# Full 128x128 matmuls for scores and AV of batches 1 to 3, with block-diagonal queries and zero-padded exponentials

## The chip, the cores and the metric

One core of a Trainium2 chip runs the whole program. The metric is the time of one execution on the device in microseconds (us). Its engines work side by side, each through its own instructions in program order, and wait for one another by semaphores: TensorE (PE, with its weight loads as PEld), VectorE (DVE), ScalarE (ACT), GpSimd (POOL) and SyncE (SP), which here only issues DMAs.

## The reference

Sparse attention over 4 batches of 8 heads, 768 positions of 64 elements, and then a feed-forward layer with a gated activation. Each query sees the keys closer than 16 positions, and one summary per block of 32 keys: the block's maximum as key and its mean as value.

```python
k_sum = k.reshape(B, H, nb, block, D).max(axis=3)      # block 32, nb 24
v_sum = v.reshape(B, H, nb, block, D).mean(axis=3)
scores_l = scale * q @ k.T                             # kept where |i - j| < 16
scores_s = scale * einsum('bhsd,bhnd->bhsn', q, k_sum) + log(block)
a = softmax(concatenate([scores_l, scores_s]))
x = (a @ concatenate([v, v_sum])).transpose(0, 2, 1, 3).reshape(B * S, H * D)
h = x @ w_in                                           # 512 -> 2048
out = (h * sigmoid(beta * h)) @ w_out                  # 2048 -> 512
```

q, k, v and the weights come as float32; the matmuls run in bfloat16.

## The kernel before

Two heads share the 128 partitions, 64 elements each, so the 8 heads are 4 pairs (`g`). Queries are cut into 12 tiles of 64 (`QT`), six in each half `u`. For a tile, the 96 keys of its window and the 24 summary keys make one set of 120 rows, held in `kw[g]` with 128 columns per tile. Scores stand transposed, keys on partitions: `s` in a PSUM bank, 128 x 768 for a pair and a half. ACT takes the exponential into `e` (`weigh`), DVE multiplies by the band mask (`mask_e`), and AV uses the tile of `e` as weights against the values `ve` (even tiles) and `vo` (odd tiles, the same values shifted by 64 rows), with a column of ones that gives the sum. `norm` divides on DVE (a reciprocal and a multiplication) into `xn`; `x_dma` transposes that by DMA, issued on ACT, into `xT`. `vm_all` computes the block means on PE, `spread` copies them on DVE into the lower rows of `ve` and `vo`.

The feed-forward layer takes most of PE. `h_tile` and its like multiply by `w_in` (L600), and the multiplication by `w_out` runs as seven products of half-size blocks (`product`, L664) whose operands are differences and sums formed on DVE: `t_sb` of the weights, `s_sb` of h (`h_sums`, `tt` at L645). `gather` adds the products up into `o_sb`, and SP stores it.

The order is written out. A list `main` holds the steps of the feed-forward layer: the h of batch 0 in two halves, its output, then for batches 1 to 3 the h (16 steps) and the products (21 steps). `run` walks it and puts in side steps, each at a position from the table `AT` (4.754 is behind step 4). The attention of batch b + 1 runs as side steps of the output of batch b. Batch 1 has its queries and keys turned on PE (`qt_pe`, copied out by L371 on DVE and L368 on ACT); in batches 2 and 3 loads, casts to bf16 on POOL (`kq_cast`, through the buffers `nat`) and transposing DMAs on SP (`kq_dma`) bring them into `qn[g]` and `kT[g]`.

PSUM is divided into two single banks `one`, three pairs of banks `big`, which while products run become two more accumulators (`acc`) and two of `big`. Scores of half 0 go into `big[2]`, of half 1 into `big[1]`; AV of pair g goes into `big[1 + g % 2]`. `e` has eight buffers.

In scores, each head is a matmul of its own with 64 partitions (L439, in batch 1; L436 in the other two), in AV each tile has weights of 128x64 and writes a half of the output's partitions (L511). Batch 0 has steps of its own (`HEAD`).

Of the kernel before, what the change touches and what calls it, by code (L numbers as in the profile page):

```python
# [17 lines left out]
    'clear': [6.428, 6.644],  # L18
# [3 lines left out]
    'late': [32.254],  # L22
# [5 lines left out]
    'sc1': [28.05, 28.06, 30.05, 30.06, 31.438, 31.448, 33.219, 33.904],  # L28
    'mk1': [28.082, 28.092, 30.899, 30.909, 32.558, 32.75, 33.826, 34.448],
    'silu1': [34.957],  # L30
    'vm1': [30.622],
    'sp1': [31.039, 33.384],
    'av1': [35.473, 35.88, 37.299, 37.483],
    'xd1': [36.323, 36.794, 40.874, 39.001],
# [14 lines left out]
    'sc2': [64.902, 64.912, 67.132, 67.349, 69.423, 69.507, 71.144, 71.507],  # L49
    'mk2': [64.907, 67.547, 69.019, 69.041, 70.656, 70.74, 74.611, 74.621],  # L50
    'silu2': [83.261],
    'vm2': [69.738],
    'sp2': [70.773, 71.834],
    'av2': [73.1, 73.251, 76.15, 76.759],
    'xd2': [73.535, 75.753, 77.844, 80.713],
# [14 lines left out]
    'sc3': [100.954, 100.964, 104.012, 104.199, 106.253, 106.263, 107.654, 107.71],  # L70
    'mk3': [101.397, 102.413, 107.921, 107.97, 106.952, 108.221, 108.907, 110.666],
    'silu3': [112.501],
    'vm3': [107.308],
    'sp3': [107.454, 109.743],
    'av3': [110.088, 110.664, 114.187, 114.973],
    'xd3': [111.756, 114.644, 117.265, 117.799],
# [4 lines left out]
    'mask2': [46.27],  # L81
# [21 lines left out]
def kernel(  # L103
# [10 lines left out]
    nc = tc.nc  # L114
    ctx.enter_context(tc.manual_schedule())
    P = 128
# [8 lines left out]
    W = 16  # L125
# [17 lines left out]
    NEG = -30000.0  # L143
    assert d_model == H * D and out.shape == (B * S, d_model) and NK + nb <= P
# [104 lines left out]
    mask = const.tile([P, NT, QT], bf16, name="mask")  # L249
# [600 lines left out]
    def av_two(g, u, ts):  # L850
        for i, t in enumerate(ts):
            av_mm(0, g + i, u, t[:, 0])
# [116 lines left out]
```

## Time and profile before

| | us |
|---|---|
| median of 3 runs (lowest, highest) | 216.38 (216.24, 218.27) |
| span of the profiled execution | 213.4 |
| PE busy in that span | 202.9 (95%) |
| weight loads busy | 140.1 (66%) |
| DVE busy | 139.5 (65%) |
| ACT busy | 119.0 (56%) |
| POOL busy | 62.0 (29%) |

The span goes from the first to the last instruction that the profiler saw; the run's time includes what lies around it, so the median of the runs is 3.0 us above the span. The profile gives no other time of its own for that execution. Batch 1's attention lies at about 55 to 75 us, batch 2's at 100 to 123, and batch 3's at 145 to 168.

In a row of the timeline stand start, time, engine, line, operation, written and read tile, shape, and the number of instructions that the row merges; in brackets how long the engine had been idle and what released it. Neighbouring matmuls overlap, so that the time of a row of eight is longer than the distance to the next row.

### The profile page before, as it was taken

The page shows a single profiled execution, that of the slowest core. Times are in us where ns is not written, and L with a number is a line of the kernel's source. Part 1 is how long each engine was busy: PE and PEld are TensorE (multiplying, and loading weights), DVE is VectorE, ACT ScalarE, POOL GpSimd, SP SyncE. Part 2 cuts the span into 40 slices and gives each one's busy share as a digit, 9 for nine tenths or more (in the row PEclk, how much of TensorE's full clock was granted, in tenths as well). Part 3 has the DMA queues.
Part 4 walks back from the last instruction along what each step waited for, and adds up shares of the span by engine and source line. Part 5 has one row for each costly group of instructions (what it writes and reads, how often), then busy time and mean ns, then how long its engine had stood idle before and what let it go on. Part 6 is the DMA issues. An engine that isn't in the chain of part 4 may idle for free.

```text
span 213.4 us, 5774 instructions
## 1 busy us (share of the span) xinstructions
PE 202.9 (95%) x2393; PEld 140.1 (66%) x2393; DVE 139.5 (65%) x323; ACT 119.0 (56%) x182; POOL 62.0 (29%) x94
## 2 busy tenths in 40 slices
PE   7778999999998999999999999999999999999993
PEld 2366856565554586556888875667788855668882
DVE  4297574799839992677889920999789704464232
ACT  2246986579489121966883137778772229772210
POOL 7609990002620009423520153461600100000111
PEclk9999999999999999999999999999999999999999
DMA  6998999999877995999979999999834820000242
GB/s 119 183 219 150 185 207 207 206 208 214 113 187 199 243 202 179 236 152 202 170 152 223 194 272 272 210 193 194 123 129 27 185 99 3 0 0 3 98 98 98
DMA packets 78393, 33.92 MB, mean 159 GB/s; under 512 B 60688, under 2 KB 75424, under 8 KB 78368
## 3 DMA queue, kind: packets, MB, share of 16 engines
q1 hardware_dynamic: 61968, 23.92, 55.2%
q0 software_dynamic: 7424, 7.34, 21.4%
q10 hardware_dynamic: 8976, 2.30, 7.3%
q8 instruction: 18, 0.29, 0.6%
q14 instruction: 7, 0.06, 0.1%
HBM read 27.37 MB, written 6.29 MB: 158 GB/s over the span
## 4 chain that ended last, share of the span: by engine, by line
PE 54%; DVE 14%; DMA 14%; SPq 5%; ACT 4%; issue 4%; POOL 3%; POOLq 0%; DVEq 0%
PE big L600 18%; PE one L664 11%; PE acc L664 8%; DMA vst<-in_v_dram 8%; PE big L578 4%; PE one L615 3%; DMA krow<-in_k_dram 3%; ACT e L447 3%; DVE kw L371 2%; DVE w_out_sb L337 2%; DMA qst<-in_q_dram 2%; DVE km L357 2%; DVE e L451 2%; POOL ve L456 1%; SPq L210 1%
## 5 line engine op out<-in xcount | busy, mean ns | idle before, releaser
L600 PE MATMUL big<-xT,w_in_sb 128*128 128x384 bf16 x360 | 60.5, 326 | 0.0
L600 PEld LDWEIGHTS <-w_in_sb 128*128 128x128 bf16 x384 | 37.5, 98 | 25.1 <-issue 0.7
L611 ACT ACTIVATE h_sb<-big,beta_sb 128x768 bf16<-128x768 f32 x45 | 39.6, 904 | 25.7 <-PE big L600 25.6
L664 PEld LDWEIGHTS <-h_sb 128*128 128x128 bf16 x320 | 30.6, 98 | 4.9 <-issue 0.5
L645 POOL TENSOR_TENSOR o_sb<-p,u 128x256 f32<-128x256 f32 x10 | 7.3, 727 | 88.9 <-DVE u L645 77.0
L447 ACT ACTIVATE e<-big,bias 128x768 bf16<-128x768 f32 x32 | 27.3, 900 | 6.2 <-PE big L426 4.3
L664 PE MATMUL one<-w_out_sb,h_sb 128*128 128x256 bf16 x240 | 30.4, 273 | 0.2 <-ACT p L368 0.2
L664 PEld LDWEIGHTS <-s_sb 128*128 128x128 bf16 x240 | 23.2, 98 | 2.8
L645 DVE TENSOR_TENSOR s_sb<-h_sb 128x768 bf16<-128x768 bf16 (+2 forms) x16 | 7.8, 487 | 23.5 <-ACT h_sb L611 23.5
L645 DVE TENSOR_TENSOR u<-one,p 128x256 f32<-128x256 f32 x20 | 8.4, 422 | 15.8 <-PE one L664 15.5
L456 POOL CAST ve<-vst 128x832 bf16<-128x832 f32 (+2 forms) x16 | 14.1, 901 | 14.9 <-DMA vst<-in_v_dram 12.5
L368 ACT COPY o_sb<-one 128x256 f32<-128x256 f32 (+1 forms) x14 | 6.1, 433 | 18.4 <-PE one L664 10.0
L451 DVE TENSOR_TENSOR e<-e,mask 128x768 bf16<-128x768 bf16 x24 | 13.7, 597 | 3.9 <-ACT e L447 3.6
L615 PE MATMUL one<-w_out_sb,h_sb 128*128 128x512 bf16 x64 | 15.2, 380 | 0.0
L365 POOL COPY kw<-km 128x288 bf16<-128x288 bf16 x12 | 7.5, 628 | 24.1 <-DVE km L357 14.4
L361 DVE TENSOR_REDUCE km<-kT 128x24 bf16<-128x768 bf16 x12 | 11.2, 944 | 1.8 <-ACT kT L368 1.8
L538 DVE TENSOR_TENSOR xn<-big,r 128x768 bf16<-128x768 f32 x12 | 11.5, 957 | 0.4
L578 PE MATMUL big<-xT,w_in_sb 128*128 128x384 bf16 x64 | 11.7, 327 | 0.0
L664 PE MATMUL acc<-t_sb,h_sb 128*128 128x256 bf16 x80 | 10.9, 273 | 0.0
L568 POOL CAST qn<-qst 128x768 bf16<-128x768 f32 x8 | 7.4, 938 | 10.2 <-DMA qst<-in_q_dram 6.9
L664 PE MATMUL one<-t_sb,s_sb 128*128 128x256 bf16 x80 | 10.4, 273 | 0.0
L664 PE MATMUL acc<-t_sb,s_sb 128*128 128x256 bf16 x80 | 10.4, 273 | 0.0
(145 smaller groups left out, 309.1 us busy)
## 6 DMA issues: line engine op xcount, KB each, us to landing
out_dram<-o_sb SPq DMA_DIRECT2D x19, 256.0 KB, 2.7
vst<-in_v_dram SPq DMA_DIRECT2D x13, 336.0 KB, 5.1
kst<-in_k_dram SPq DMA_DIRECT2D x8, 384.0 KB, 5.0
qst<-in_q_dram SPq DMA_DIRECT2D x8, 384.0 KB, 4.6
w_in_sb<-in_moe_w_in_dram POOLq DMA_DIRECT2D x4, 512.0 KB, 8.0
w_out_sb<-in_moe_w_out_dram POOLq DMA_DIRECT2D x4, 512.0 KB, 13.1
vo<-ve SPq DMA_DIRECT2D x12, 107.2 KB, 2.4
vst<-in_v_dram SPq DMA_DIRECT2D x3, 416.0 KB, 7.1
```

The source lines that it names most:

```text
L361: nc.vector.tensor_reduce(out=km[g][:, NK:NK + nb], in_=kT[g][:, W:W + S].rearrange("p (n f) -> p n f", f=block), op=ALU.max, axis=AX.X)
L365: eng.tensor_copy(out=kw[g][:, :, NK:NK + nb], in_=km[g][:, None, NK:NK + nb].to_broadcast([P, NT, nb]))
L447: nc.scalar.activation(out=e[:], in_=s[:, :, 0:HS], func=ACTF.Exp, bias=bias[:, 0:1], scale=scale)
L451: nc.vector.tensor_mul(out=e.rearrange("p h (m q) -> p h m q", q=QT), in0=e.rearrange("p h (m q) -> p h m q", q=QT), in1=(mask2 if b > 1 e ...
L456: eng.tensor_copy(out=ve[:, g, lo:hi, 0:D], in_=vst[g][:, lo:hi])
L538: nc.vector.tensor_mul(out=x[:, 3 * us[0]:3 * us[0] + 3 * n].rearrange("p (k j) h d -> p k (j h) d", k=n), in0=tv[:, :, :, 0:D], in1=r[:, ...
L578: nc.tensor.matmul(t[:, 0:HS], w_in_sb[:, ki, i * P:(i + 1) * P], xT[:, ki, 0:HS], start=(ki == 0), stop=(ki == k1 - 1))
L600: nc.tensor.matmul(o, w_in_sb[:, ki, i * P:(i + 1) * P], x, start=(ki == 0), stop=(ki == k1 - 1))
L611: nc.scalar.activation(out=o, in_=t, func=ACTF.Silu, scale=beta_sb[:, i:i + 1])
L615: nc.tensor.matmul(t[:, 0:hi - lo], h_sb[:, n, ms * P:(ms + 1) * P], w_out_sb[:, n, lo:hi], start=(n == 0), stop=(n == k2 - 1))
L645: eng.tensor_tensor(out=o, in0=a, in1=b, op=op)
L664: nc.tensor.matmul(SLOTS[n], a[:, j, t * P:(t + 1) * P], b[:, j], start=(j == 0 and n not in (2, 3, 7)), stop=(j == J2 - 1), skip_group_ch ...
```

## The change

Scores become one matmul for both heads. A tile `qz` of 128 x 2 x 4 x 768 holds the queries block-diagonally: copy 0 has the first head in partitions 0 to 63 and zeros below, copy 1 the second head in partitions 64 to 127 and zeros above. The weights are all 128 rows of `kw` for the tile, the 128 columns of the moving side are 64 queries of one head and 64 of the other. `qn[g]` is now a view of copy 0.

The exponentials live in five fixed tiles `epad` of 6 x 3 x 64: the middle block of each three is zero. AV takes as weights 128 columns that begin with the even tile and end in zeros, or begin with zeros and end with the odd tile, so that both add up in the same full output. The tiles are handed out from a list `free_e` and given back where AV has been issued.

So that `qz` is filled, `qt_pe` copies half a partition range at a time, alternately by DVE and ACT, and turns into `big[1]` and `big[0]`. In batches 2 and 3 the transposing DMA still writes both heads into copy 0; `q_fix` then moves the second head into copy 1 (DVE) and clears its place (POOL). Zeros are set by a memset at the start, by `clear_q` (two memsets of 64 x 1536) and by `clear_e`. The mask has 14 tiles instead of 12, ordered for the new layout, and its turned copy for batches 2 and 3 (`turn_mask`) is made ahead of batch 1 (position 6.9 instead of 46.27). The pools `nat` and `op` go from 5 to 4 and from 4 to 3 buffers, and the eight buffers of `e` go. Positions in `AT` of scores, masks, means, spreads, AV and `x_dma` change, mostly to earlier ones, and AV of one pair now stands among the scores of later pairs; `qf2` and `qf3` are new.

```diff
@@ AT (a few of its lines) @@
-    'clear': [6.428, 6.644],
+    'clear': [5.9, 6.644, 6.9, 6.1, 7.2, 7.3],
...
-    'sc2': [64.902, 64.912, 67.132, 67.349, 69.423, 69.507, 71.144, 71.507],
+    'sc2': [64.902, 64.912, 66.6, 66.61, 69.423, 70.5, 71.8, 72.6],
...
-    'av2': [73.1, 73.251, 76.15, 76.759],
+    'av2': [70.1, 71.6, 73.9, 75.8],
...
-    'mask2': [46.27],
+    'qf2': [58.2, 59.6, 60.6, 66.9],
+    'qf3': [94.5, 95.5, 95.9, 97.5],
@@ -141,14 +142,14 @@
     k2 = d_ff // P
     VW = D + 2
     NEG = -30000.0
+    NE = 5
     assert d_model == H * D and out.shape == (B * S, d_model) and NK + nb <= P
 
     const = ctx.enter_context(tc.tile_pool(name="consts", bufs=1))
     stage = ctx.enter_context(tc.tile_pool(name="stage", bufs=7))
-    natp = ctx.enter_context(tc.tile_pool(name="nat", bufs=5))
-    ep = ctx.enter_context(tc.tile_pool(name="ep", bufs=8))
+    natp = ctx.enter_context(tc.tile_pool(name="nat", bufs=4))
     xp = ctx.enter_context(tc.tile_pool(name="xp", bufs=4))
-    op = ctx.enter_context(tc.tile_pool(name="op", bufs=4))
+    op = ctx.enter_context(tc.tile_pool(name="op", bufs=3))
     ps = ctx.enter_context(tc.tile_pool(name="ps", bufs=1, space=bass.MemoryType.PSUM))
 
     one = [ps.tile([P, 1, 512], f32, name=f"one{i}") for i in range(2)]
...
-    mask = const.tile([P, NT, QT], bf16, name="mask")
+    mask = head.tile([P, NT + 2, QT], bf16, name="mask")
...
@@ -292,16 +293,23 @@
     select(band[:], 2 * W - 1, [[1, QT]], -1)
 
     def more_masks():
-        nc.vector.tensor_copy(out=mask[:], in_=band[:, None, :].to_broadcast([P, NT, QT]))
-        nc.vector.memset(mask[0:W, 0], 0.0)
-        nc.gpsimd.affine_select(out=mask[:, NT - 1], in_=mask[:, NT - 1], compare_op=ALU.is_ge, fill=0.0,
-                                base=QT + W - 1, pattern=[[0, QT]], channel_multiplier=-1)
+        nc.vector.tensor_copy(out=mask[:], in_=band[:, None, :].to_broadcast([P, NT + 2, QT]))
+        nc.vector.memset(mask[0:W, 0:2], 0.0)
+        nc.gpsimd.affine_select(out=mask[:, NT:], in_=mask[:, NT:], compare_op=ALU.is_ge, fill=0.0,
+                                base=QT + W - 1, pattern=[[0, 2], [0, QT]], channel_multiplier=-1)
         nc.vector.memset(mask[NK:NK + nb], 1.0)
 
-    mask2 = const.tile([P, NT, QT], bf16, name="mask2")
+    mask2 = const.tile([P, NT + 2, QT], bf16, name="mask2")
 
     def turn_mask():
         nc.vector.tensor_copy(out=mask2.rearrange("p m (c f) -> p m c f", c=2), in_=mask.rearrange("p m (f c) -> p m c f", c=2))
+
+    def clear_q(gs):
+        nc.vector.memset(qz[D:P, 0, gs], 0.0)
+
+    def clear_e():
+        for t in epad:
+            nc.vector.memset(t[:, :, 1], 0.0)
 
     def clear_kw():
         for g in range(G):
@@ -309,7 +317,10 @@
             nc.vector.memset(kw[g][:, NT - 1, QT + W:NK], 0.0)
             nc.vector.memset(kw[g][:, :, NK + nb:P], 0.0)
 
-    qn = [const.tile([P, S], bf16, name=f"qn{g}") for g in range(G)]
+    qz = const.tile([P, 2, G, S], bf16, name="qz")
+    qn = [qz[:, 0, g] for g in range(G)]
+    epad = [const.tile([P, 2 * 3, 3, QT], bf16, name=f"ep{i}") for i in range(NE)]
+    nc.vector.memset(qz[0:D, 1], 0.0)
...
-    def qt_pe(b, gs, bg, cps):
+    def qt_pe(b, gs, bg):
         ts = [turned(qrow, b, big[bg][:, i], g) for i, g in enumerate(gs)]
-        for g, t, cp in zip(gs, ts, cps):
-            cp(qn[g].rearrange("p (f c) -> p f c", c=CS[b]), t.rearrange("p c f -> p f c"))
+        for g, t in zip(gs, ts):
+            for h, cp in enumerate((dve_cp, act_cp)):
+                r = slice(h * D, (h + 1) * D)
+                cp(qz[r, h, g].rearrange("p (f c) -> p f c", c=CS[b]), t[r].rearrange("p c f -> p f c"))
+
+    def q_fix(g):
+        nc.vector.tensor_copy(out=qz[D:P, 1, g], in_=qz[D:P, 0, g])
+        nc.gpsimd.memset(qz[D:P, 0, g], 0.0)
 
 
     et, turns = {}, {}
 
     def q_tile(g, h, m):
         return qn[g][h * D:(h + 1) * D, m * QT:(m + 1) * QT]
-
...
@@ -430,26 +443,40 @@
         s = big[bg]
         for j in range(HT):
             m = u * HT + j
-            for h in range(2):
-                o = s[:, h, j * QT:(j + 1) * QT]
-                if b > 1:
-                    nc.tensor.matmul(o.rearrange("p (c f) -> p c f", c=2), kw[g][h * D:(h + 1) * D, m, :], q_tile2(g, h, m),
-                                     start=True, stop=True)
-                else:
-                    nc.tensor.matmul(o, kw[g][h * D:(h + 1) * D, m, :], q_tile(g, h, m), start=True, stop=True)
+            o, q = s[:, j % 2, j // 2 * P:(j // 2 + 1) * P], qz[:, :, g]
+            if b > 1:
+                o = o.rearrange("p (h c f) -> p h c f", h=2, c=2)
+                q = q.rearrange("p h (j c f) -> p h j c f", c=2, f=P)[:, :, m // 4, :, m % 4 * 32:m % 4 * 32 + 32]
+            else:
+                o = o.rearrange("p (h f) -> p h f", h=2)
+                q = q[:, :, m * QT:(m + 1) * QT]
+            nc.tensor.matmul(o, kw[g][:, m, :], q, start=True, stop=True)
         turns["s", g, u] = s
         weigh(b, g, u)
 
+    free_e = list(range(NE))
+
+    def release(b, g, u):
+        free_e.append(et.pop((b, g, u))[0])
+
     def weigh(b, g, u):
         s = turns.pop(("s", g, u))
-        e = ep.tile([P, 2, HS], bf16, name="e", tag="e")
-        et[(b, g, u)] = e
-        nc.scalar.activation(out=e[:], in_=s[:, :, 0:HS], func=ACTF.Exp, bias=bias[:, 0:1], scale=scale)
+        n = free_e.pop(0)
+        t = epad[n]
+        if b == 0:
+            e = t.rearrange("p a b q -> p (a b q)")[:, 0:2 * HS].rearrange("p (h s) -> p h s", h=2)
+            o, i = e, s[:, :, 0:HS]
+        else:
+            e, o, i = t, blocks(t), s[:, :, 0:HS].rearrange("p b (a q) -> p b a q", q=QT)
+        et[(b, g, u)] = n, e
+        nc.scalar.activation(out=o, in_=i, func=ACTF.Exp, bias=bias[:, 0:1], scale=scale)
+
+    def blocks(t):
+        return t[:, :, 0:3:2].rearrange("p a b q -> p b a q")
 
     def mask_e(b, g, u):
-        e = et[(b, g, u)]
-        nc.vector.tensor_mul(out=e.rearrange("p h (m q) -> p h m q", q=QT), in0=e.rearrange("p h (m q) -> p h m q", q=QT),
-                             in1=(mask2 if b > 1 else mask)[:, None, u * HT:(u + 1) * HT, :].to_broadcast([P, 2, HT, QT]))
+        e = blocks(et[(b, g, u)][1])
+        nc.vector.tensor_mul(out=e, in0=e, in1=(mask2 if b > 1 else mask)[:, 2 * u:2 * u + NT].rearrange("p (b a) q -> p b a q", b=2))
 
 
     def v_cast(eng, g, lo=0, hi=JV):
@@ -500,9 +527,9 @@
     xn = {}
     AVW = 3 * 2 * (D + 1)
 
-    def av_mm(b, g, u, t):
+    def av_mm0(g, u, t):
         tv = t[:, 0:AVW].rearrange("p (j h e) -> p j h e", j=3, h=2)
-        e = et[(b, g, u)]
+        e = et[(0, g, u)][1]
         for j in range(3):
             J = 3 * u + j
             for h in range(2):
@@ -510,10 +537,21 @@
                     lo = (2 * j + par) * QT
                     nc.tensor.matmul(tv[par * QT:(par + 1) * QT, j, h], e[:, h, lo:lo + QT],
                                      (vo if par else ve)[:, g, h * J6 + J, 0:D + 1], start=True, stop=True)
+        release(0, g, u)
+
+    def av_mm(b, g, u, t):
+        tv = t[:, 0:AVW].rearrange("p (j h e) -> p j h e", j=3, h=2)
+        e = et[(b, g, u)][1].rearrange("p a b q -> p a (b q)")
+        for j in range(3):
+            for h in range(2):
+                for par in range(2):
+                    nc.tensor.matmul(tv[:, j, h], e[:, 2 * j + h, par * QT:par * QT + P],
+                                     (vo if par else ve)[:, g, h * J6 + 3 * u + j, 0:D + 1], start=(par == 0), stop=(par == 1))
+        release(b, g, u)
 
...
...
@@ -902,12 +941,11 @@
     at("av0", [lambda: av_two(0, 1, one), lambda: av_two(2, 1, one[1:]), lambda: av_two(3, 1, one[:1])])
     at("x0", [lambda: x_two(0, 1, dve_cp, one[0]), lambda: x_two(2, 1, dve_cp, one[1])])
     at("scale", [lambda i=i: scale4(i) for i in range(4)])
-    at("clear", [clear_kw, more_masks])
+    at("clear", [clear_kw, more_masks, turn_mask, clear_e, lambda: clear_q(slice(0, 2)), lambda: clear_q(slice(2, 4))])
     at("kt", [lambda i=i: kt_pe(1, (2 * i, 2 * i + 1), 1 + i, dve_cp) for i in range(2)])
     at("km", [lambda g=g: km_pe(g, nc.gpsimd) for g in range(G)])
-    at("qt", [lambda i=i: qt_pe(1, (2 * i, 2 * i + 1), 1 + i, (dve_cp, act_cp)) for i in range(2)])
+    at("qt", [lambda i=i: qt_pe(1, (2 * i, 2 * i + 1), 1 - i) for i in range(2)])
     at("late", [late_tiles])
-    at("mask2", [turn_mask])
...
+            at("qf" + n, [lambda g=g: q_fix(g) for g in range(G)])
             at("win" + n, [lambda g=g: windows_nat(dve_cp, g) for g in range(G)])
             at("kx" + n, [lambda g=g: key_max_nat(g) for g in range(G)])
             at("ks" + n, [lambda g=g: key_sums(nc.gpsimd, g) for g in range(G)])
```

Three places show how instructions move. The first is DVE ahead of batch 1's first masks. Before (`big1` and `big2` hold turned queries, `e_1156` is the first tile of exponentials):

```order
L645 TENSOR_TENSOR t_sb_189<-w_out_sb_184 128x2048
L357 TENSOR_REDUCE km3_130<-kw3_119 128x24
L645 TENSOR_TENSOR t_sb_189<-w_out_sb_184,t_sb_189 128x2048
L371 COPY qn0_177<-big1_80 128x768
L371 COPY qn2_179<-big2_81 128x768
L451 TENSOR_TENSOR e_1156<-e_1156,mask_111 128x768
L451 TENSOR_TENSOR e_1170<-e_1170,mask_111 128x768
```

Now, with `ep4_179` as the first tile of exponentials:

```order
L684 TENSOR_TENSOR t_sb_189<-w_out_sb_184 128x2048
L368 TENSOR_REDUCE km3_127<-kw3_116 128x24
L684 TENSOR_TENSOR t_sb_189<-w_out_sb_184,t_sb_189 128x2048
L382 COPY qz_174<-big1_77 64x768 x2
L382 COPY qz_174<-big0_82 64x768 x2
L479 TENSOR_TENSOR ep4_179<-ep4_179,mask_108 128x2x6x64
```

Two copies of whole query pairs have become four of half the partitions, and ACT has the other four. Further up on DVE, between the masks and the scaling of `w_out`, stands the turned mask and the clearing of `qz`:

```order
L296 COPY mask_108<-band_107 128x896
L297 MEMSET mask_108 16x64
L300 MEMSET mask_108 24x896
L305 COPY mask2_173<-mask_108 128x896
L308 MEMSET qz_174 64x768 x2
L348 TENSOR_SCALAR w_out_sb_184<-w_out_sb_184,inv_beta_186 128x512 x4
```

Before, the rows L296 to L300 stood there as L295 to L299, with `w_out`'s scaling directly behind them.

The second place is PE in batch 1, where AV of a pair ends. Before, behind AV of pair 1 in `big2`:

```order
L511 MATMUL big2_81<-ve_120,e_1209 64x65
L511 LDWEIGHTS e_1209
L511 MATMUL big2_81<-vo_121,e_1209 64x65
L615 LDWEIGHTS h_sb_182
L615 MATMUL one1_79<-w_out_sb_184,h_sb_182 128x512
```

Now, behind AV of pair 0 in `big1`:

```order
L548 MATMUL big1_77<-ve_117,ep2_177 128x65
L548 LDWEIGHTS ep2_177
L548 MATMUL big1_77<-vo_118,ep2_177 128x65
L453 LDWEIGHTS kw2_115
L453 MATMUL big1_77<-qz_174,kw2_115 128x128
```

The products that stood behind AV stand later; the scores of pair 2 (`kw2`) follow, into the bank into which AV has just written.

The third place is DVE in batch 2, at the last sums of h that the products need. Before:

```order
L645 TENSOR_TENSOR s_sb_1302<-h_sb_182 128x768
L645 TENSOR_TENSOR s_sb_1302<-s_sb_1302,h_sb_182 128x768
L645 TENSOR_TENSOR s_sb_1302<-h_sb_182,s_sb_1302 128x768
L645 TENSOR_TENSOR h_sb_182<-h_sb_182 128x2x384
L371 COPY kw2_118<-kT2_125 128x12x96
L361 TENSOR_REDUCE km2_129<-kT2_125 128x24
```

Now:

```order
L382 COPY kw2_115<-kT2_122 128x12x96
L415 COPY qz_174<-qz_174 64x768 x2
L372 TENSOR_REDUCE km2_126<-kT2_122 128x24
L684 TENSOR_TENSOR s_sb_1388<-h_sb_182 128x384
L684 TENSOR_TENSOR s_sb_1388<-s_sb_1388,h_sb_182 128x384
L684 TENSOR_TENSOR s_sb_1388<-h_sb_182,s_sb_1388 128x384
```

The copies of L415 are `q_fix`; two of them stand between the keys' copy and their maximum, ahead of the last sums. The first of them stands ahead of the third group of sums.

More of the change, by code (lines that the diff above doesn't have):

```diff
@@ L21 @@
     'qt': [26.508, 26.967],
-    'late': [32.254],
+    'late': [35.9],
     'ws': [23.447, 26.164, 38.352, 39.431],
@@ L570, in kq_dma @@
     def kq_dma(nm, b, g):
-        t = kT[g][:, W:W + S] if nm == "k" else qn[g][:]
+        t = kT[g][:, W:W + S] if nm == "k" else qn[g]
         nc.sync.dma_start_transpose(out=t.rearrange("p (j t) -> p j t", j=J6),
```

38 lines of the change are left out of this document (18 added, 20 removed).

## The prediction

> **What bounds the kernel now.** I read the busy shares first, then the stretches around the edited work, then the waits of TensorE, then the timelines.
>
> ```profile
> span 213.4 us, 5774 instructions
> PE 202.9 (95%) x2393; PEld 140.1 (66%) x2393; DVE 139.5 (65%) x323; ACT 119.0 (56%) x182; POOL 62.0 (29%) x94
> 50.00:58.00 8.00, 7.98 (x98) 4.37 (x96) 8.00 (x14) 4.81 (x8) 3.68 (x5) 1.00 1.09 156
> 58.00:81.00 23.00, 21.75 (x326) 13.86 (x325) 17.95 (x38) 12.47 (x20) 2.58 (x5) 1.00 0.87 195
> 100.00:116.00 16.00, 16.00 (x282) 12.99 (x280) 14.57 (x34) 11.82 (x19) 5.08 (x6) 1.00 0.89 183
> 140.00:160.00 20.00, 19.83 (x301) 14.88 (x298) 16.98 (x37) 15.28 (x23) 6.79 (x9) 1.00 0.88 160
> PE big L439 <- ACT qn L368: 0.6, 1, 0.6
> PE big L439 <- ACT e L447: 0.4, 1, 0.4
> PE big L511 <- DVE e L451: 0.2, 1, 0.2
> ```
>
> The stretches list length, then busy time of PE, weight loads, DVE, ACT and POOL. TensorE bounds everything: it is 95% busy, and in the stretches that hold the scores and the AV of batches 2 and 3 it loses 0.0 of 16 and 0.2 of 20 us. Its waits at the edited instructions come to 1.2 us in all. So there is nearly nothing to win in waits, and whatever new wait TensorE gets is paid in full. DVE has no slack from 50 to 58 us, where batch 1 begins: it is busy 8.00 of 8.00.
>
> **Term 1: TensorE's own work.** Three rows of TensorE's timeline (start, time, instructions), then three pieces of the chain:
>
> ```profile
> 105.42 1.04 PE L664 MATMUL one<-w_out_sb,h_sb 128*128 128x256 bf16 x8
> 106.39 0.52 PE L436 MATMUL big<-qn,kw 64*128 64x64 bf16 x24
> 106.84 1.05 PE L664 MATMUL one<-w_out_sb,h_sb 128*128 128x256 bf16 x8
> 68.60 0.88 PE big L511 x48
> 167.67 0.33 PE big L560 x6
> 23.71 0.19 PE one L519 x6
> ```
>
> Eight products take 0.87 when others follow. From 105.42 to 106.84 are 1.42, so 24 small score matmuls, which serve two steps, cost 0.55, with about 0.10 of change-over in it. They become 12 with 128x128 weights and 128 columns; six such (L560) take 0.33, so 0.66: +0.11, twelve times, +1.3. AV: 48 small matmuls, two head pairs, take 0.88, so one pair 0.49 with its change-over; it becomes 24 with full weights and 65 columns, six of which (L519) take 0.19: 0.74. +0.25, twelve times, +3.0. Sum **+4.3**; ends 2 (no change-over saved, weight loads hidden better) and 5.
>
> **Term 2: the start of batch 1.** Before:
>
> ```profile
> 38.14 0.56 DVE L371 COPY xT<-one 128x768 bf16<-128x768 bf16 x1 [0.72 <-PE one L860]
> 56.20 1.81 DVE L371 COPY qn<-big 128x768 bf16<-128x768 bf16 x2
> 57.18 1.66 ACT L368 COPY qn<-big 128x768 bf16<-128x768 bf16 x2 [2.86 <-DVE qn L371]
> 58.73 0.59 ACT L368 COPY o_sb<-one 128x512 f32<-128x512 f32 x1
> 59.28 1.69 ACT L447 ACTIVATE e<-big,bias 128x768 bf16<-128x768 f32 x2
> 61.18 0.52 PE L439 MATMUL big<-qn,kw 64*128 64x64 bf16 x24
> L304 DVE COPY mask<-mask 128x768 bf16<-128x768 bf16 x1 | 0.6, 550 | 0.0
> L232 DVE MEMSET blank<- 128x256 uint32 x1 | 0.3, 272 | 0.9 <-PEq L953 0.9
> L261 DVE MEMSET edge<- 128x128 uint32 x1 | 0.2, 165 | 0.0
> ```
>
> DVE gets, ahead of the query copies: the mask turn 0.57 (it stood after batch 1, and is 896 wide now), two clears of qz of 768 words (0.272 and 0.165 at 256 and 128 words give 0.7 each, 1.35), and the widened mask 0.2. Five clears of e (192 words, 0.2 each) fall almost wholly into DVE's idle time ahead of the two xT copies (0.72 in this row); 0.2 is left of them and of hand-overs. Together +2.3, and no slack to take it. The copies then begin at 58.5. They become eight halves that differ in partitions, not in elements per lane, so each keeps its 0.95 (DVE) or 0.80 (ACT); each ACT half waits for DVE's, and DVE's second for ACT's first, as all write qz. Two such ladders end near 58.5 + 6.3 = 64.8. The o_sb copy follows on ACT, and the first exponentials run 65.3 to 67.1. Scores of pair 1, at 61.18 before, wait for each of the two banks in turn: 66.25 and 67.1 instead, with nothing else of TensorE between. **+6.0**. Ends: 3 (the additions alone, with a little handing over) and 7.
>
> **Term 3: scores behind the norm.** The diff's order puts scores of pair 2 directly behind AV of pair 0 in the same bank, and scores of pair 3 directly behind AV of pair 1. A bank must be normalised before it is overwritten:
>
> ```profile
> 115.32 0.23 DVE L537 RECIPROCAL r<-big 128x12 f32<-128x12 f32 x1
> 115.58 0.96 DVE L538 TENSOR_TENSOR xn<-big,r 128x768 bf16<-128x768 f32 x1
> 112.45 0.63 DVE L496 COPY vo<-vm_sb 32x768 bf16<-32x768 bf16 x2
> ```
>
> That is 1.2, with 0.25 of hand-overs 1.45, while TensorE has nothing it may run. A mask (0.6) or the two spreads (1.2) ahead on DVE make it 2.0 to 2.65. Walking DVE's new order: batch 1 1.45 and 2.4, batch 2 2.0 and 1.7, batch 3 2.65 (once; there AV follows the scores). **+10.2**; ends 6 and 12.
>
> **Term 4: AV behind the last exponentials.**
>
> ```profile
> 104.14 1.70 ACT L447 ACTIVATE e<-big,bias 128x768 bf16<-128x768 f32 x2
> L451 DVE TENSOR_TENSOR e<-e,mask 128x768 bf16<-128x768 bf16 x24 | 13.7, 597 | 3.9 <-ACT e L447 3.6
> 116.57 1.28 ACTq L553 DMA_TRANSPOSE xT<-xn  x1
> ```
>
> The exponential of the last step (0.85) and its mask (0.6) stand behind an issue of xT on ACT (1.28), which now lies between the exponentials of pair 3. AV of pair 2 comes after a few products, and waits 1.3, 1.6 and 1.0 in the three batches, **+3.9**; ends 1 and 5.
>
> **Term 5: means and spreads.**
>
> ```profile
> L645 DVE TENSOR_TENSOR u<-one,p 128x256 f32<-128x256 f32 x20 | 8.4, 422 | 15.8 <-PE one L664 15.5
> ```
>
> The value means follow product 7 directly, into the bank that the product's sum still fills, and wait for DVE's u and o_sb (0.42 each) and what is ahead: 2.15 and 1.95 in batches 2 and 3. The first AV waits for the spreads: 1.35, 0.3 and 1.05. **+6.8**; ends 3 and 8.
>
> **Term 6: q_fix ahead of the sums.**
>
> ```profile
> 100.33 2.76 SPq L572 DMA_TRANSPOSE qn<-qn  x2
> qn<-qn SPq DMA_TRANSPOSE x8, 3.5
> 103.28 0.36 DVE L645 TENSOR_TENSOR s_sb<-h_sb,s_sb 128x384 bf16<-128x384 bf16 x1
> 103.66 1.05 PE L664 MATMUL one<-t_sb,s_sb 128*128 128x256 bf16 x8
> 140.12 3.89 SPq L572 DMA_TRANSPOSE qn<-qn  x3
> L361 DVE TENSOR_REDUCE km<-kT 128x24 bf16<-128x768 bf16 x12 | 11.2, 944 | 1.8 <-ACT kT L368 1.8
> ```
>
> Before, the last sum ends at 103.64 and product 6 takes it at 103.66. Now copies of qz for pairs 1 and 2 stand on DVE between the sums, and wait for transposes that are issued at 100.33 and 101.7 and land 3.5 later, at 103.8 and 105.2. A key maximum (0.94) and two groups of four sums (0.36 each, 2.8) follow: product 6 at about 108.8 by the old clock, less what TensorE has to do meanwhile, 4.3. In batch 3 all three copies stand ahead of the sums; with four natural-layout buffers instead of five the fourth cast comes later too: 5.65. The loads of q queue on SP behind stores of the stage before, so they shift with a late stage, but not wholly: DMA gets time to catch up. I take 8 of the 9.95. Ends 0 (landed in time) and 11.
>
> The waits of before at these places go, 1.2, and with those of products beside them about **−2**. Sum: 4.3 + 6.0 + 10.2 + 3.9 + 6.8 + 8.0 − 2.0 = **+37.2**. The profiled span of 213.4 becomes 250.6. The median of the runs, 216.38, is 3.0 above that span; I keep it: **253.6 us**. The padding memsets, the mask's broadcast (same 768 elements) and POOL's q_fix memset (POOL is 29% busy) I cost at nothing; POOL's would cost its own length if a v cast behind it came late, which is inside term 5's upper end.
>
> **The rivals.**
> A: the stalls are real but q_fix is not one, because the transposes land before DVE reaches them. For: DMA gains some 12 us of time per stalled stage. Against: SP's loads of q stand behind stores of o_sb. 253.6 − 8.0 = 245.6.
> B: the waits are mostly covered by products that TensorE can run meanwhile, and only term 1 and the ladder's additions remain: 216.4 + 4.3 + 3 − 2 = 221.7. Against: TensorE's order has nothing between AV and scores.
> C: not slower. Small and full matmuls no longer alternate, and these rows show what the weight loads lose ahead of the small ones:
>
> ```profile
> L439 PEld LDWEIGHTS <-kw 64*128 64x128 bf16 x96 | 1.9, 94 | 3.0 <-issue 2.9
> L436 PEld LDWEIGHTS <-kw 64*128 64x128 bf16 x192 | 3.3, 95 | 1.6 <-issue 1.5
> L511 PEld LDWEIGHTS <-e 128*64 128x64 bf16 x336 | 6.5, 111 | 3.6 <-issue 1.6 <-DVE e L451 0.7 <-DVE ve L496 0.6
> ```
>
> If all 6.0 of "issue" came off TensorE's path with the 2.0 of waits, against 4.3 more work, and every stall were covered: 216.4 − 3.7 = 212.7. It decides only if terms 2 to 6 together stay under 4. Against: weight loads overlap matmuls, and a change-over shows as 0.10 in term 1's rows. The Trainium skill, TensorEngine Tiling (Array Packing), Key Properties, says that "Changing tiling mode (not just tile) drains the TensorE"; the 0.10 there is what such a drain could be. By that rule the change saves it at each score and AV step; term 1 has counted it.
> D: the clock. All stretches above show 1.00. If the two waits of 4 us or more in term 6 each halved the clock for as long again, eight products of 0.87 would take 1.74, some 2 to 4 us more in each batch: 253.6 + 6 = 259.6. The Trainium skill, TensorE: Matmul & The Clock Gate, Part 1, says that about 3.4 us of idleness halves the clock until about 3.4 us of busy time have passed. No row of before can show it.
>
> **How the numbers follow.** The forecast gets 0.50, A 0.25, D 0.10, B 0.12 and C 0.03. All low ends at once would make 229, all high ends 262. That every one of six is low is unlikely, so the range begins at 234, which holds A; it ends at 263, which holds D. What it leaves out is B, C and part of the forecast's own low side: **234 to 263**. A measurement of this kernel tells about 1% from no change (214.2 to 218.5); only C, half within 1% and half under, falls there: faster 0.02, same 0.02, slower 0.96.
>
> **What would show it.** Right: scores (now L453) at 0.66 for twelve and AV (L548) at 0.74 for 24; TensorE's busy share falling from 95% to near 83%, with its waits led by L453 for DVE's xn, the value means for o_sb, product (L703) for s_sb, and L548 for ACT's e; first exponential of batch 1 near 65; stages beginning at about 93, 150 and 207 instead of 80, 125 and 171. Wrong: scores of pair 2 starting without a wait (term 3), q_fix copies that show no idle time for a DMA ahead of them (term 6, rival A), or a granted clock under 1.00 behind the waits (rival D).

## The result and the profile after

The changed kernel takes 258.86 us (median of 4, 256.74 to 266.49) against 216.45. One of the four, 266.49, fell into a slower state that executions of any kernel fall into now and then, so the ratio and all differences below go by the others, with a median of 257.9. The ratio is 1.191, with an interval of 1.181 to 1.201. The change makes the kernel slower by 41.4 us; the forecast was 253.6, in a range of 234 to 263. The profiled execution took 259.84, with a span of 258.1.

The page's row of the engines, the row of the granted clock in 40 slices, and the list of what TensorE waited for (us in total, times, longest):

```profile
PE 219.3 (85%) x2244; PEld 153.8 (60%) x2249; DVE 151.0 (58%) x341; ACT 122.0 (47%) x184; POOL 66.0 (26%) x102
PEclk9999999997776999999599999999598999999999
PE one L703 <- DVE s_sb L684: 11.5, 5, 3.5
PE big L453 <- DVE xn L577: 8.7, 5, 2.6
PE big L453 <- ACT qz L379: 3.6, 2, 2.3
PE acc L512 <- DVE o_sb L684: 2.1, 2, 1.1
PE big L548 <- ACT ep L472: 1.7, 2, 1.0
PE big L548 <- DVE ve L523: 1.5, 2, 0.9
```

TensorE is idle for 38.8 us instead of 10.5, and 29.1 of that stand in these six rows, all at instructions that the change edits, moves, or makes wait for a later input. It is busy for 16.4 us more, with the clock below full in several slices, so that not all of that is more work. An estimate divides it: the busy time of each half microsecond times the clock granted in it, summed up, is what the work would take at full clock. That is 207.8 us, against 202.9 before, where the clock was full throughout. So 4.9 of the 16.4 are more work, and 11.5 are the lower clock.

Where the time went is read from the rows in which the h of batches 1, 2 and 3 begins, before (L600) and after (L639):

```profile
80.39 1.46 PE L600 MATMUL big<-xT,w_in_sb 128*128 128x384 bf16 x8
125.09 1.46 PE L600 MATMUL big<-xT,w_in_sb 128*128 128x384 bf16 x8
170.46 1.46 PE L600 MATMUL big<-xT,w_in_sb 128*128 128x384 bf16 x8
```

```profile
93.63 1.46 PE L639 MATMUL big<-xT,w_in_sb 128*128 128x384 bf16 x8
153.56 1.46 PE L639 MATMUL big<-xT,w_in_sb 128*128 128x384 bf16 x8
215.15 1.46 PE L639 MATMUL big<-xT,w_in_sb 128*128 128x384 bf16 x8
```

The loss is 13.2 up to the first, then 15.2 and 16.2, and nothing behind the last: 42.9 of span are left before, 42.9 after. It lies in the three stretches that hold the attention of batches 1 to 3, and the prediction's 93 for the first was hit, its 150 and 207 missed by 4 and 8. By the same estimate the lower clock takes 5.4, 2.9 and 3.2 us of the three stretches. The prediction had put it at nothing, so even the hit is partly luck: without the clock's 5.4 the first stretch lost 7.8 us, not 13.

### The profile page after: what moved, and what is told of

It is laid out like the page before. It is cut to its first block, busy times and chain, and to the rows that moved or that the text cites. A ratio compares the mean times of both kernels' runs of the same rounds, so it can differ in the third digit from the quotient of the medians.

```text
span 258.1 us, 5529 instructions
## 1 busy us (share of the span) xinstructions
PE 219.3 (85%) x2244; PEld 153.8 (60%) x2249; DVE 151.0 (58%) x341; ACT 122.0 (47%) x184; POOL 66.0 (26%) x102
## 4 chain that ended last, share of the span: by engine, by line
PE 62%; DVE 19%; DMA 10%; ACT 4%; issue 2%; POOL 1%; ACTq 1%; POOLq 0%; DVEq 0%
PE big L639 20%; PE one L703 12%; PE acc L703 9%; DMA qz<-qn 5%; PE big L617 4%; PE one L654 4%; PE big L453 3%; PE big L548 3%; DMA krow<-in_k_dram 3%; DVE s_sb L684 2%; DMA vst<-in_v_dram 2%; ACT ep L472 2%; DVE xn L577 2%; DVE kw L382 2%; DVE w_out_sb L348 2%
## 5 line engine op out<-in xcount | busy, mean ns | idle before, releaser
L639 PE MATMUL big<-xT,w_in_sb 128*128 128x384 bf16 x360 | 60.5, 326 | 0.0
L639 PEld LDWEIGHTS <-w_in_sb 128*128 128x128 bf16 x384 | 37.6, 98 | 25.0 <-issue 0.7
L472 ACT ACTIVATE ep<-big,bias 128x768 bf16<-128x768 f32 x32 | 28.1, 900 | 26.5 <-PE big L453 21.9
L453 PE MATMUL big<-qz,kw 128*128 128x128 bf16 x144 | 14.2, 252 | 12.4 <-DVE xn L577 8.7
L703 PE MATMUL one<-t_sb,s_sb 128*128 128x256 bf16 x80 | 12.4, 292 | 11.5 <-DVE s_sb L684 11.5
L453 PEld LDWEIGHTS <-kw 128*128 128x128 bf16 x144 | 12.1, 115 | 15.6 <-issue 14.6
L479 DVE TENSOR_TENSOR ep<-ep,mask 128x768 bf16<-128x768 bf16 x24 | 13.0, 553 | 12.9 <-ACT ep L472 12.7
L654 PE MATMUL one<-w_out_sb,h_sb 128*128 128x512 bf16 x60 | 17.7, 436 | 0.5 <-issue 0.4
L548 PEld LDWEIGHTS <-ep 128*128 128x128 bf16 x288 | 11.1, 100 | 6.1 <-issue 3.0
L379 ACT COPY p<-acc 128x256 f32<-128x256 f32 x10 | 3.7, 372 | 22.6 <-PE acc L703 22.0
L548 PE MATMUL big<-ve,ep 128*128 128x65 bf16 x144 | 11.3, 197 | 3.4 <-ACT ep L472 1.7
```

Source lines behind the costliest of these rows:

```text
L453: nc.tensor.matmul(o, kw[g][:, m, :], q, start=True, stop=True)
L472: nc.scalar.activation(out=o, in_=i, func=ACTF.Exp, bias=bias[:, 0:1], scale=scale)
L479: nc.vector.tensor_mul(out=e, in0=e, in1=(mask2 if b > 1 else mask)[:, 2 * u:2 * u + NT].rearrange("p (b a) q -> p b a q", b=2))
L548: nc.tensor.matmul(tv[:, j, h], e[:, 2 * j + h, par * QT:par * QT + P], (vo if par else ve)[:, g, h * J6 + 3 * u + j, 0:D + 1], start=(par ...
L639: nc.tensor.matmul(o, w_in_sb[:, ki, i * P:(i + 1) * P], x, start=(ki == 0), stop=(ki == k1 - 1))
L654: nc.tensor.matmul(t[:, 0:hi - lo], h_sb[:, n, ms * P:(ms + 1) * P], w_out_sb[:, n, lo:hi], start=(n == 0), stop=(n == k2 - 1))
```

## The experiments

Times below are medians; the changed kernel has 257.9, the kernel before 215.5 to 216.5 beside the runs. The interval of the changed kernel's ratio is 4 us wide, so a difference of 1 or 2 us tells little. The same holds for one stretch of two traces: from the h of batch 1 to that of batch 2 the changed kernel takes 59.9 us, and the run with matmuls of zeros, which has no edit there, 58.0.

**q_fix behind the sums.**

```diff
-    'qf2': [58.2, 59.6, 60.6, 66.9],
+    'qf2': [63.42, 64.95, 67.0, 69.3],
-    'qf3': [94.5, 95.5, 95.9, 97.5],
+    'qf3': [99.85, 101.0, 103.1, 105.2],
```

> The changed kernel with q_fix of batches 2 and 3 moved behind the sums of h that product 6 needs (just ahead of each pair's scores), nothing else. The prediction's term 6: product 6's waits for s_sb (11.5 us in the changed kernel, 5 times) go to under 1.5, the clock stays at 1.00 behind them, and at most 2 us come back as waits of the scores for q_fix's copies: 258.9 - 10 = 247 to 251. Rival, the sums are late for another reason (the stage's h, or the key work on VectorE): the waits for s_sb stay above 6 us and the time within 2.5 us of 258.9. Rival, the wait is only moved to the scores: time within 3 us of 258.9 with L453 waiting for q_fix or its DMA.

259.3 us (ratio 1.192 to 1.207): nothing gained. TensorE's waits and the longest of them:

```profile
PE big L453 <- POOL qz L416: 8.3, 3, 5.6
179.39 1.44 PE L453 MATMUL big<-qz,kw 128*128 128x128 bf16 x12 [5.61 <-POOL qz L416]
```

The waits for s_sb are gone, and the scores wait instead, for GpSimd's zeros. In the wait shown, VectorE's copy ran at 176.46, behind its sums, and the zeros at 178.60, behind a value cast and a copy on GpSimd. The third reading held, the wait only moved: the place of q_fix among the sums was not the whole of the cost, its chain through two queues was.

**Query copies divided by PSUM tile.**

```diff
-            for h, cp in enumerate((dve_cp, act_cp)):
+            for h in range(2):
...
-    at("qt", [lambda i=i: qt_pe(1, (2 * i, 2 * i + 1), 1 - i) for i in range(2)])
+    at("qt", [lambda i=i: qt_pe(1, (2 * i, 2 * i + 1), 1 - i, (act_cp, dve_cp)[i]) for i in range(2)])
```

> The changed kernel with the eight half copies of batch 1's queries divided by the PSUM tile that they read: ScalarE takes pairs 0 and 1, VectorE pairs 2 and 3. In the changed kernel they alternate on each PSUM tile, and VectorE's second copy starts when ScalarE's first ends. If it is two engines reading one PSUM tile that makes them take turns, ScalarE starts at about 56.5 and is done near 60, the first exponential of batch 1 starts at 60 to 61.5 instead of 65.4, TensorE's 3.6 us of waits of L453 for ScalarE's qz go to under 1, and the half clock from 62 to 67 is gone: 258.9 - 5 to - 8, 251 to 254. If it is the common output tile qz that orders them (what the prediction said), the two engines still take turns and nothing moves by over 1 us.

253.9 us (1.162 to 1.188). First the changed kernel, copies of both engines and the first exponentials, then this run's copies, first exponentials and the start of the next h:

```profile
58.67 0.95 DVE L382 COPY qz<-big 64x768 bf16<-64x768 bf16 x1
59.65 0.79 ACT L379 COPY qz<-big 64x768 bf16<-64x768 bf16 x1 [5.42 <-DVE qz L382]
60.47 1.82 DVE L382 COPY qz<-big 64x768 bf16<-64x768 bf16 x2 [0.86 <-ACT qz L379]
61.45 1.66 ACT L379 COPY qz<-big 64x768 bf16<-64x768 bf16 x2 [1.02 <-DVE qz L382]
65.43 3.48 ACT L472 ACTIVATE ep<-big,bias 128x768 bf16<-128x768 f32 x4
```

```profile
55.27 3.22 ACT L379 COPY qz<-big 64x768 bf16<-64x768 bf16 x4 [1.48 <-PE big L395]
58.25 3.85 DVE L382 COPY qz<-big 64x768 bf16<-64x768 bf16 x4
59.00 1.70 ACT L472 ACTIVATE ep<-big,bias 128x768 bf16<-128x768 f32 x2
87.11 1.46 PE L639 MATMUL big<-xT,w_in_sb 128*128 128x384 bf16 x8
```

In the changed kernel each engine copies half of each of the pairs 0 to 3, and ScalarE, idle for 5.42 us, starts only behind VectorE's first copy. VectorE's copies of pairs 1 and 2 run back to back (1.82 for two), the latter at the same time as ScalarE's of pair 1. Those two read different PSUM tiles and both write qz; the engines take turns only where they read one tile. With a tile each, VectorE starts before ScalarE is done and waits for nothing. But the two hardly overlap: what is won is that ScalarE begins at 55.27, when the queries have just been turned, and not behind VectorE, which other work holds until 58.25. The exponentials begin 6.4 us earlier and batch 1 ends 6.5 earlier, of which 4.0 are left in the time.

**The matmuls' shape alone.** The order of work, copies, q_fix and memsets are the changed kernel's.

```diff
-            nc.tensor.matmul(o, kw[g][:, m, :], q, start=True, stop=True)
+            for h in range(2):
+                ...
+                nc.tensor.matmul(o, kw[g][h * D:(h + 1) * D, m, :], q, start=True, stop=True)
...
-                    nc.tensor.matmul(tv[:, j, h], e[:, 2 * j + h, par * QT:par * QT + P],
+                    nc.tensor.matmul(tv[par * QT:(par + 1) * QT, j, h], e[:, 2 * j + par, 2 * h],
```

> The changed kernel in its order of work, with its copies, q_fix and memsets, but scores as 64-partition matmuls of one head (24 for what are 12) and AV with 64 columns of weights writing half the partitions, as before. It tells the shape of the matmuls from the order of the work. Term 1: -4.3 of the 42 us, 254 to 256; every wait stays. Rival, full matmuls are the cause: at least half of the 42 us goes, under 238.

259.5 us (1.190 to 1.209). The shape is not what costs here, and term 1 doesn't show either. TensorE is busy for 2.8 us less and idle for 3.6 more. The two largest waits grew, from 11.5 and 8.7:

```profile
PE one L703 <- DVE s_sb L684: 13.1, 5, 5.4
PE big L453 <- DVE xn L577: 10.8, 5, 2.8
```

What TensorE saves it waits for longer. That VectorE and the DMAs set the time there is the likely reason; no run shows it apart.

**Matmuls of zeros in batch 1's first wait.**

```diff
+            at("fill", [lambda: warm(10, big[2][:, 0])])
```

> The changed kernel with ten matmuls of zeros (128x128 weights, 512 columns, 0.23 us each) put ahead of the first scores of batch 1, into the bank that these scores write next, so that TensorE is busy where it waits 2.3 us for the first copies. Rival D, idleness halves the clock: the granted clock from 63 to 67 goes from 0.50 to 1.00, the eight products there from 3.62 to 1.9, and batch 1 ends 1.5 to 2.5 us sooner, the whole 256 to 257.5. If the half clock does not come from the idleness, the clock stays at 0.50 there and the time within 1 us of 258.9.

The four times spread from 255.0 to 261.6, too far to say whether this is faster; the stretch from 63 to 67 us tells more (length, then PE, weight loads, DVE, ACT, POOL, clock, DMA), first of the changed kernel, then of this one:

```profile
63.00:67.00 4.00, 4.00 (x15) 1.68 (x14) 1.51 (x2) 2.96 (x5) 0.00 (x0) 0.50 0.14 52
```

```profile
63.00:67.00 4.00, 2.22 (x14) 1.11 (x14) 1.00 (x2) 2.89 (x6) 0.10 (x1) 1.00 0.00 0
93.28 1.46 PE L640 MATMUL big<-xT,w_in_sb 128*128 128x384 bf16 x8
```

The clock is 1.00 with the gap filled. Five other runs that leave it open (q_fix late, small matmuls, no q_fix, positions moved, matmuls in product 6) all have half the clock from between 60.6 and 62.7 us on. So idleness had halved it, as rival D and the Trainium skill (TensorE: Matmul & The Clock Gate, Part 1) have it, though behind a gap of 2.31 us.

The half clock did not go, it moved: here it comes from 68.1 to 71.5, behind a wait of 1.86 us for the exponentials. Batch 1 ends 0.35 us sooner, which tells nothing, as runs without an edit up to there end it between 92.1 and 94.2. So the 1.5 to 2.5 expected did not show, and the run does not say what a full clock would be worth.

**No q_fix.**

```diff
-            at("qf" + n, [lambda g=g: q_fix(g) for g in range(G)])
```

> The changed kernel without q_fix in batches 2 and 3: the second head's queries are not moved and its place is not zeroed, so that part of the computation is left out; all matmuls, exponentials and stores stay. The run with q_fix behind the sums showed its wait moved to the scores, which then wait for GpSimd's zeros. If q_fix's chain (transposing DMA, copy on VectorE, zeros on GpSimd) is what costs, both waits go: product's waits for s_sb from 11.5 to under 1.5 without the scores' waits coming up by over 1.5, time 247 to 250. If the DMA's lateness itself is the cost, scores wait for the transposes instead and the time stays above 254. If GpSimd slows VectorE, the four last sums of h in batch 2, 0.9 to 1.0 us each beside GpSimd's casts and zeros, come back to 0.36 with the zeros gone.

This kernel leaves the second head's queries of batches 2 and 3 where they are. 246.8 us (1.141 to 1.152): -11.1, just under the 247 to 250 expected. No wait for s_sb is left, none of the scores for queries in batches 2 and 3, and only one neighbour grew by more than 1 us, by 1.7:

```profile
PE acc L512 <- DVE o_sb L684: 3.8, 2, 2.0
```

**Positions moved apart** (some of batch 2's shown; the other batches' alike, and a few steps of batch 1 beside them).

```diff
-    'sc2': [64.902, 64.912, 66.6, 66.61, 69.423, 70.5, 71.8, 72.6],
+    'sc2': [64.902, 64.912, 66.6, 66.61, 69.423, 73.5, 74.9, 76.4],
-    'vm2': [68.2],
+    'vm2': [69.2],
-    'av2': [70.1, 71.6, 73.9, 75.8],
+    'av2': [71.6, 72.9, 78.2, 79.2],
```

> The changed kernel with the positions of AV, later scores, masks, means, spreads and x_dma moved apart: one to three products now stand between AV of a pair and the scores that write its bank, between the last exponentials and AV, and between product 7 and the value means (behind product 3, as before). Nothing else changes but the positions of late_tiles and of the first sums behind the masks. Terms 3 to 5: the waits L453 for xn (8.7), L512 for o_sb (2.1), L548 for ACT's ep (1.7) and for the spreads (1.5) fall together from 14.0 to under 5, and the time by as much and by the half clock behind them: 244 to 251. Rival: the last x_dma now land too late and the next h waits for them (L617 or L639 for a DMA), which gives back more than half: 253 to 259.

244.5 us (1.129 to 1.140): -13.4. The scores' waits for xn are gone altogether, L512 waits 0.2, L548 3.5 in sum: 14.0 became 3.7. That is 10.3 us of waits; by the estimate of busy time and clock, the lower clock takes 6.6 us here instead of 11.5, which makes up the rest. The late x_dma did not hold the next h.

**The three together**, and **the three with small matmuls**.

> The three together: query copies divided by PSUM tile, positions moved apart, no q_fix (its part of the computation left out). Full 128x128 matmuls stay. If the three groups of waits are the whole loss and only term 1 (4.3) and VectorE's additions stay: 220 to 226, clock at 1.00 throughout. If the waits are replaced by others (x_dma late, ScalarE's exponentials as the bound): 230 or more.

> The same three with scores and AV as 64-partition and 64-column matmuls again. In the changed kernel this substitution moved the time by nothing, beside waits that TensorE would have had anyway. With the waits gone term 1 must show: 4.3 us under the run with the full matmuls, 2.5 to 5.5. Rival: full matmuls cost nothing even then (within 1 us), so that term 1 was wrong and not hidden.

225.7 us (1.044 to 1.053) and 224.0 (1.033 to 1.042), both without q_fix's part of the work. TensorE's row of the first, then TensorE's row and largest waits of the second in what the change touches:

```profile
PE 209.9 (92%) x2249; PEld 149.8 (66%) x2249; DVE 148.1 (65%) x333; ACT 124.0 (55%) x186; POOL 61.7 (27%) x94
```

```profile
PE 206.9 (92%) x2393; PEld 141.1 (63%) x2393; DVE 148.0 (66%) x333; ACT 123.8 (55%) x186; POOL 62.2 (28%) x94
PE acc L512 <- DVE o_sb L684: 2.1, 2, 1.1
PE big L548 <- DVE ve L523: 1.8, 2, 1.2
PE big L548 <- ACT ep L472: 1.8, 1, 1.8
PE big L512 <- DVE qz L382: 1.0, 1, 1.0
```

The three parts alone gave 4.0, 11.1 and 13.4, in sum 28.5; together they give 32.2. So none of them is a part of another; the 3.7 on top are little more than such a sum is good for. Now the shape seems to count: 1.7 us between the medians, and 3.0 us less busy TensorE. By the intervals it may be 0.5 to 4.4, which holds term 1's 4.3 only just.

**A complete kernel, mended.** The first two edits, q_fix in other places, and its zeros on VectorE.

```diff
-    'qf2': [58.2, 59.6, 60.6, 66.9],
+    'qf2': [62.1, 64.95, 67.0, 69.3],
-    'qf3': [94.5, 95.5, 95.9, 97.5],
+    'qf3': [98.9, 101.0, 103.1, 105.2],
...
-        nc.gpsimd.memset(qz[D:P, 0, g], 0.0)
+        nc.vector.memset(qz[D:P, 0, g], 0.0)
```

> A complete kernel with full 128x128 matmuls: query copies divided by PSUM tile, positions moved apart, and q_fix kept, but pair 0's set ahead of the last group of sums and the others just ahead of their scores, with the zeros on VectorE instead of GpSimd. The same without q_fix took 226.4. If q_fix's price was its place in two queues (ahead of the sums on VectorE, behind value casts on GpSimd), little of the 12 us comes back: 227 to 232. If the transposes are too late for any copy behind them, scores wait for q_fix: 234 to 240.

233.5 us (1.071 to 1.087), between the two cases. Both have a part: scores wait 3.1 for q_fix, and TensorE's wait for the spreads, which stand behind it on VectorE, is 3.5 instead of 1.9.

```profile
PE big L548 <- DVE ve L523: 3.5, 3, 1.6
PE big L453 <- DVE qz L416: 3.1, 2, 2.4
```

It takes back 24 of the 41 us with all of the work done, and is still about 17 above the kernel before.

**Matmuls of no use in product 6's waits.**

```diff
+            if n == 6 and t == 0 and j in (6, 7) and ...:
+                for _ in range((24, 22)[j - 6]):
+                    nc.tensor.matmul(one[1][:, 0, DH:2 * DH], identity, w_out_sb[:, 0, 0:DH], ...)
```

> The changed kernel with 24 and 22 extra matmuls of 256 columns (0.11 us each) ahead of the last two matmuls of product 6 in batches 2 and 3, into columns of its bank that nothing reads, where TensorE waits 2.5 to 3.5 us for s_sb. If idleness halves the clock and this costs time where TensorE is the bound behind the wait: the clock from 124 to 130 and from 185 to 190 is 1.00 instead of 0.58 and 0.77, eight products there take 1.04 again and not 1.91, and the time is 3 to 5 us lower, 254 to 256. If the time behind the wait is set by other engines, as in batch 1, the clock is 1.00 and the time within 1.5 us of 258.9.

256.9 us (1.172 to 1.204). The extra matmuls stand within product 6's sum, in its bank, and spoil the output; the work of the kernel is all there. The stretch from 124 to 130 us and the wait of the value means, of the changed kernel and then of this one:

```profile
124.00:130.00 6.00, 5.78 (x35) 4.26 (x33) 4.53 (x11) 2.44 (x4) 0.79 (x2) 0.56 0.63 146
130.82 0.58 PE L512 MATMUL acc<-ve,A_avg 128*32 128x128 bf16 x28 [1.04 <-DVE o_sb L684]
```

```profile
124.00:130.00 6.00, 3.62 (x61) 2.98 (x59) 4.86 (x12) 2.23 (x5) 1.82 (x3) 1.00 0.60 146
128.23 0.58 PE L512 MATMUL acc<-ve,A_avg 128*32 128x128 bf16 x28 [2.38 <-DVE o_sb L684]
```

The clock is full. The value means begin 2.6 us sooner, 0.9 of which this trace had at the end of batch 1, ahead of any edit, and 1.3 us more go into their wait. Later, from 191.6 to 198.4, the clock is at half again. 1.0 us are left in the time, which its spread does not tell from nothing.

## Why the prediction was right, and where it was not

**What bounds.** Right: nothing was to be won in waits, and the new waits were paid. What came is the forecast's waits, smaller than forecast, with rival D's clock on top. The time, 257.9, lies nearer to D's 259.6 than to the forecast's 253.6, and the clock under 1.00 behind the waits is one of the prediction's own signs of being wrong. By span, with the estimate above for the split of the busy time:

| us | forecast | trace |
|---|---|---|
| TensorE's own work (term 1) | 4.3 | 4.9 |
| waits (terms 2 to 6, less the 2.0 that go) | 32.9 | 28.3 |
| lower clock | 0 | 11.5 |
| sum | 37.2 | 44.7 |

The profiled execution lies 2.0 above the median, so its sum is larger than the 41.4 of the times. The step that failed is to put the clock at nothing in the sum. That the number still came within 4.3 us is partly luck, as the waits were over-sized by 4.6.

**Term 1**, 4.3: the durations were right. Rows of the changed kernel, six scores until the next row, and a pair's AV in the chain:

```profile
191.06 0.51 PE L453 MATMUL big<-qz,kw 128*128 128x128 bf16 x6
191.40 1.04 PE L703 MATMUL acc<-w_out_sb,s_sb 128*128 128x256 bf16 x8
85.22 0.73 PE big L548 x24
```

0.34 for six and 0.73 for 24 were forecast as 0.33 and 0.74. What failed is its place in the sum: taking the work away gave nothing in the time here, as TensorE then waited longer, and 1.7 where the waits were gone.

**Term 2**, 6.0: the copies went as forecast (first exponential at 65.43 for 65.3), but TensorE's waits there were 3.6, with the half clock behind them. Dividing the copies by tile gave 6.5 at the end of batch 1 and 4.0 in the time. The reason was wrong: the copies take turns because they read one PSUM tile, not because they write qz.

**Terms 3 to 5**, 20.9: every kind of wait named was there, though not in every batch, and most were over-sized. Measured: 8.7 for 10.2, 1.7 for 3.9, 3.6 for 6.8, in sum 14.0; moving the positions apart took 10.3 of these away and gave 13.4 back, clock included. In batch 1 neither wait for the norm was over 1.32, as the second spreads ended when AV did; for pair 3 the forecast was 2.4.

**Term 6**, 8.0: too small, 11.5 of waits and 11.1 without q_fix. The step that failed is "DMA gets time to catch up", which took 9.95 to 8. The copies found the transposes still missing; the pair of them that was issued at 100.33 before was issued 12.9 later, of the 13.2 by which the stage was late, and in batch 3 the three of 140.12 came 28.9 later, where the stage was 28.5 late. The longest wait of VectorE, 4.99, is at pair 0's copy, which the prediction's walk of batch 2 had not counted. Copies, and TensorE's wait behind them:

```profile
113.25 2.56 SPq L611 DMA_TRANSPOSE qz<-qn  x2
113.40 0.36 DVE L415 COPY qz<-qz 64x768 bf16<-64x768 bf16 x1 [4.99 <-DMA qz<-qn]
175.01 0.88 DVE L415 COPY qz<-qz 64x768 bf16<-64x768 bf16 x2 [1.39 <-DMA qz<-qn]
123.38 0.39 PE L703 MATMUL one<-t_sb,s_sb 128*128 128x256 bf16 x1 [2.50 <-DVE s_sb L684]
```

The parts that the runs took away make 4.0 + 13.4 + 11.1 + 1.7 = 30.2 of the 41.4 us one by one, and 33.9 together. The run with the three edits and small matmuls is still 8.5 above the kernel before beside it. Its trace has 6.7 us of waits in the four rows shown. The moves alone had taken the wait for o_sb down to 0.2, and without q_fix it came back; the wait for query copies came with dividing them by tile; those for spreads and exponentials the moves had never taken away. No run takes apart VectorE's added masks and zeros, the smaller buffer pools or the five tiles for exponentials, so what makes up the rest stays open.

**The rivals.** A was wrong (the transposes had not landed). B and C never came near. D's mechanism is shown, and at more places than it named: the clock is at half from 61.0 to 67.8, 74.6 to 81.5, 122.4 to 129.2, 180.4 to 187.3 and 197.5 to 200.9 us. By the estimate that lengthens TensorE's work by 11.5 us, not 6. How much of it would come back with the waits kept and the clock full is open: filling single waits changed the time by nothing that its spread lets one tell, as the half clock moved elsewhere and other waits grew.

## What to carry to other kernels

On an engine without slack, read a reordering by what stands directly behind each instruction in its queue: a bank that is written right behind its use waits for the whole reading chain, and here that cost more than the change of the matmul's shape. Fix-up steps behind a late transfer cost their chain, not their length, and moving them alone moved the wait. Sum up an engine's work, its waits and its clock separately: new waits lowered the clock of the work behind them, and work that was saved came back as waits.

## What the runs showed of the hardware

VectorE's sums of two SBUF inputs slow down while GpSimd casts. Sums of 128x384 take 0.36 alone; in the changed kernel, then without q_fix, beside GpSimd's row:

```profile
121.35 1.02 DVE L684 TENSOR_TENSOR s_sb<-h_sb 128x384 bf16<-128x384 bf16 x1
122.41 0.91 DVE L684 TENSOR_TENSOR s_sb<-s_sb,h_sb 128x384 bf16<-128x384 bf16 x1
121.16 2.90 POOL L483 CAST ve<-vst 128x832 bf16<-128x832 f32 x3
```

```profile
117.38 0.92 DVE L684 TENSOR_TENSOR s_sb<-h_sb,s_sb 128x384 bf16<-128x384 bf16 x1
117.16 2.83 POOL L483 CAST ve<-vst 128x832 bf16<-128x832 f32 x3 [0.95 <-PE one L703]
```

So for the sums it is the casts and not q_fix's zeros, which the second run has not. A sum beside a memset alone kept its 0.36:

```profile
120.00 0.73 POOL L416 MEMSET qz<- 64x768 bf16 x1
120.18 0.36 DVE L684 TENSOR_TENSOR s_sb<-s_sb,h_sb 128x384 bf16<-128x384 bf16 x1
```

The Trainium skill, SBUF — State Buffer, section "SBUF: two separate sides", has a port pair that such an operation and a GpSimd operation that reads SBUF hold in turn, each for its whole length; these rows agree in that a sum beside casts takes about as long as a cast (0.97 each). Copies with one input slow down too, and beside zeros as well: one of `q_fix` took 0.79 beside a memset at 117.65 (0.36 elsewhere), the keys' copy 1.13 beside a cast in the run without q_fix (0.45 elsewhere). A change that delays sums into the casts pays for it: in batch 2 the two sums shown first are 1.2 us longer than alone, ahead of product 6's second wait of 2.50.

The clock fell to half behind gaps that I had not counted as long enough. TensorE's first wait of batch 1 in the changed kernel:

```profile
60.49 0.49 PE L453 MATMUL big<-qz,kw 128*128 128x128 bf16 x6 [2.31 <-ACT qz L379]
```

It is shorter than the 3.4 us that the Trainium skill (TensorE: Matmul & The Clock Gate, Part 1) gives for an idle window, and yet the clock was at half from 60.98 to 67.80. All ten changes of the clock in this trace lie on one grid of 3.41 us. The step of the grid ahead of the first fall, and one that no fall followed:

```profile
57.57:60.98 3.41, 1.08 (x8) 0.57 (x8) 2.55 (x4) 0.79 (x1) 3.30 (x4) 1.00 0.02 4
132.66:136.07 3.41, 1.77 (x34) 1.55 (x31) 3.28 (x11) 1.27 (x2) 0.00 (x0) 1.00 1.05 238
```

TensorE is idle for 2.33 us of the first and 1.64 of the second. In the traces of the changed kernel and seven of the runs, all 28 steps at full clock with at least 1.9 us of idle time were followed by half the clock, and none with less than 1.2; in between both happen. So it is not one long gap that counts, but the idle time within a step, and where a wait falls on the grid, which differs between executions.
